# Two-branch attention: PE transposes replaced by normalising in the transposed layout through DRAM, dense pieces re-planned, output projections deferred

## The chip, the cores and the metric

One core of a Trainium2 chip runs the whole program. The metric is the device time of one execution in microseconds (us); the time before is the median of three runs, 526.55 us (526.25 to 527.35).

## What is computed

Two attention branches read their own input of 2048 rows by 640 columns (bf16, 32 heads of 20), and their outputs stand side by side in one 2048 x 1280 result. Cut to what matters:

```
A:  for each of 4 segments s of 512 rows:
      a_dot = softmax(q k^T * scale + causal mask within s) v
      a_mem = (phi(q) M) / (phi(q) z + 1e-6)        # M, z from earlier segments; phi(t) = t+1 if t>0 else exp(t)
      o     = g * a_mem + (1 - g) * a_dot           # g = sigmoid(beta), one per head
      M, z += phi(k)^T v, sum of phi(k)
    out_A = concat(o) @ wo
B:  out_B = softmax over a causal sliding window of 256 keys (q k^T * scale) v @ wo
```

## The kernel before, in words

The work goes in eight phases, B0 A0 B1 A1 B2 A2 B3 A3, one for each branch and chunk of 512 rows. A phase has 20 packs (A, and B0) or 24 packs (B1 to B3); a pack is scored for two pairs of heads. For each pair `scores` (L375) writes a PSUM tile Sc of 128 x 1024 (two of them exist) with matmuls that use 20 rows of the array, ACT takes its exponential into pt (L380, "an exp" below; 344 in all), and DVE (L393, branch B) or POOL (L397, L402) masks blocks of pt. `weigh` (L423) then multiplies by V with four matmuls of 32 columns side by side, into the only tile O. The v tiles carry a column of ones, so that row 20 of each head's group of 32 in O is the softmax's denominator. When a group of four heads (a unit, eight in a phase) is done, DVE copies O to oc (L435), PE transposes oc block by block (L442), and DVE takes the reciprocal of the denominators (L445) and multiplies (L450) into o_tok, which has tokens on the partitions.

Everything else is a list of dense pieces ("atoms") that `run` doles out between the packs, in the proportion of their costs: the projections of the next phase (k and q, five times five matmuls of 512 columns each, L189; v, eight times five of 320 columns, L209), the memory of branch A (phi, L281 to L283; reading M, L306 to L316; transposing phi(k), L326, and updating M, L337 to L348), and the output projection of the phase before (transposing o_tok, L242, copying it, L246, five matmuls of 320 columns each, L253, copying, L256, storing, L260). All of these write PSUM tiles called D, of which there are three; DVE empties them. k and q go through DRAM once to put each head on its own 32 partitions: written by L195 (kd, qd), read back by L200 in four DMAs (kp, qp). Every DMA is issued by SP, in order, and an issue that has to wait holds up all behind it.

The order on each engine is not the order of the code: the tile framework's scheduler fixes a list of instructions for each engine when the program is built, and each engine then works its list off in order. The lists that the section on the change shows are these.

Of the kernel before, what the change touches and what calls it, by code (L numbers as in the profile page):

```python
# [80 lines left out]
class Kern:  # L81

    def __init__(self, ctx, tc, ins, out2d):
# [10 lines left out]
        self.xT, self.qc, self.kc, self.qp, self.kp, self.o_tok = {}, {}, {}, {}, {}, {}  # L94
        self.omem = None
# [12 lines left out]
    def setup(self):  # L108
# [11 lines left out]
        self.w["Aq"] = self.load_w("wAq", ins["A_wq"])  # L120
        self.w["Av"] = self.load_w("wAv", ins["A_wv"])
        self.w["Bo"] = self.load_w("wBo", ins["B_wo"])
        self.w["Ao"] = self.load_w("wAo", ins["A_wo"])
# [13 lines left out]

        bm = cp.tile([P, KT, 8], F32, name="bmask")
        nc.vector.memset(bm[:], 1.0)
        for m in range(KT):  # L140
            off = P * m - DH * (P * m // DH)
            nc.gpsimd.affine_select(out=bm[:, m, :], in_=bm[:, m, :], pattern=[[-DH, 8]],
                                    compare_op=ALU.is_ge, fill=0.0, base=off,
                                    channel_multiplier=1)
            nc.gpsimd.affine_select(out=bm[:, m, :], in_=bm[:, m, :], pattern=[[DH, 8]],
                                    compare_op=ALU.is_ge, fill=0.0, base=DH - 1 - off,
                                    channel_multiplier=-1)
        self.bm = bm
# [20 lines left out]
        self.ge, self.omg = ge, omg  # L169
        self.macc = cp.tile([P, KT, 8, DH + 1], F32, name="macc")  # L170
        self.mz = cp.tile([P, KT, 8, DH + 1], BF16, name="mz")
# [5 lines left out]
    def atoms_qkv(self, br, c):  # L177
# [4 lines left out]
        def proj(which, m):  # L182
            if m == 0:
                t = self.io.tile([P, KT, CH], BF16, name="%sc%s" % (which, br), bufs=1)
                (self.qc if which == "q" else self.kc)[br] = t
# [7 lines left out]
            if m == KT - 1:  # L193
                sc = self.dram.tile([KT * P, CH], BF16, name="%sd%s" % (which, br), bufs=2)
                nc.sync.dma_start(out=sc[:].rearrange("(m p) s -> p m s", p=P), in_=t[:])  # L195
                pt = self.io.tile([P, G, CH], BF16, name="%sp%s" % (which, br),
                                  bufs=2 if (which == "k" and br == "B") else 1)
                src = sc[:].rearrange("(g j d) s -> j d g s", g=G, j=4)
                for j in range(4):
                    nc.sync.dma_start(out=pt[32 * j:32 * j + DH, :, :], in_=src[j])  # L200
                if which == "q":
                    self.qp[br] = pt
                else:
                    self.kp[br, c] = pt
# [21 lines left out]
        for tt in range(CT):  # L226
            for hf in range(2):
                out.append((0.8, lambda tt=tt, hf=hf: vproj(tt, hf)))
        return out

    def atoms_out(self, br, c):
        nc = self.nc
        out = []
        st = {}

        def tr(tt):
            if br == "A" and c > 0 and tt == 0:
                nc.vector.tensor_tensor(out=self.o_tok["A"][:], in0=self.o_tok["A"][:],
                                        in1=self.omem[:], op=ALU.add)
            pT = self.dtile([P, KT, P], BF16)  # L240
            for m in range(KT):
                nc.tensor.transpose(out=pT[:, m, :],  # L242
                                    in_=self.o_tok[br][:, tt, m * P:(m + 1) * P],
                                    identity=self.ident[:])
            oT = self.wk.tile([P, KT, P], BF16, name="oT", bufs=2)
            nc.vector.tensor_copy(out=oT[:], in_=pT[:])  # L246
            st["oT"] = oT
# [318 lines left out]
```

## Time and profile before

| what | value |
|---|---|
| median of three runs | 526.55 us |
| the profiled execution's own time | 526.12 us |
| its span, first to last instruction | 524.0 us |
| busy: PE, DVE, ACT, POOL | 479.0, 348.4, 348.0, 205.3 us |
| mean granted TensorE clock | 0.847 |
| DMA: packets, bytes, share of 16 engines | 52,163, 38.71 MB, 27.7% |

The span is what the views below divide up; the execution's own time has another 2.1 us around it. "Busy" of PE counts overlapping matmuls once. A phase begins with its first exp; in the profile that is at 40.3, 90.9, 142.9, 202.3, 266.7, 327.5, 392.0 and 450.8 us, and the last exp ends at 503.0. The granted clock is 1.00 or 0.50 at any moment, and a stretch's figure is the mean of these.

### The profile page before, as it was taken

The numbers are of one execution on the slowest core, as the hardware profiler recorded it, in microseconds if no ns is written. First come the engines' busy times: TensorE is split into PE (matmuls) and PEld (weight loads), VectorE is DVE, ScalarE is ACT, GpSimd is POOL, SyncE is SP. The second block draws the span as 40 slices with busy tenths as digits, with TensorE's granted clock in tenths as the row PEclk, the third lists the DMA queues.
The fourth block names the chain that finished last, engine by engine and source line by source line (L and its number), as shares of the span: only waits on it lengthen the run. The fifth ranks groups of instructions, "written<-read, shape, count | busy, mean of one in ns | idle before, by whom it ended". The sixth has DMA issues, their size and how long they took to land.

```text
span 524.0 us, 10856 instructions
## 1 busy us (share of the span) xinstructions
PE 479.0 (91%) x4182; PEld 210.8 (40%) x4208; DVE 348.4 (66%) x886; ACT 348.0 (66%) x376; POOL 205.3 (39%) x498
## 2 busy tenths in 40 slices
PE   3947999999998999999999899999999899999975
PEld 1522234345533444454443344344453344433323
DVE  2753569557589996565579997556649977743343
ACT  0016669578789878675479878667448968977630
POOL 1002223346455444453345345344325544554420
PEclk9985569999999799995699789997589979955568
DMA  8993303454113230431013421150010430000001
GB/s 245 322 224 62 100 2 102 81 142 83 45 41 99 71 77 26 137 88 29 14 39 99 102 53 39 64 135 18 1 40 23 115 78 28 26 0 14 27 13 51
DMA packets 52163, 38.71 MB, mean 74 GB/s; under 512 B 22416, under 2 KB 52112, under 8 KB 52112
## 3 DMA queue, kind: packets, MB, share of 16 engines
q1 hardware_dynamic: 52112, 38.03, 27.7%
q8 instruction: 33, 0.54, 0.4%
q14 instruction: 18, 0.15, 0.1%
HBM read 17.05 MB, written 15.73 MB: 63 GB/s over the span
## 4 chain that ended last, share of the span: by engine, by line
PE 69%; DVE 17%; ACT 6%; DMA 4%; issue 2%; SPq 1%; POOL 0%; ACTq 0%; DVEq 0%
PE Sc L375 18%; PE D L189 13%; PE D L253 11%; PE O L423 11%; PE D L209 6%; ACT pt L380 6%; DVE pt L393 5%; PE D L442 4%; DVE oc L435 3%; DVE phi L283 2%; DMA qdB<-qcB 2%; PE D L337 1%; DVE qcA L192 1%; PE D L242 1%; PE D L326 1%
## 5 line engine op out<-in xcount | busy, mean ns | idle before, releaser
L380 ACT ACTIVATE pt<-Sc 128x1024 bf16<-128x1024 f32 (+1 forms) x344 | 332.0, 1015 | 125.2 <-PE Sc L375 88.7
L402 POOL TENSOR_SCALAR_AFFINE_SELECT pt<-pt 128x256 bf16<-128x256 bf16 x224 | 103.0, 470 | 163.8 <-ACT pt L380 158.4
L397 POOL TENSOR_SCALAR_AFFINE_SELECT pt<-pt 128x256 bf16<-128x256 bf16 x256 | 99.8, 408 | 134.1 <-ACT pt L380 130.5
L393 DVE TENSOR_TENSOR pt<-pt,cmask 128x256 bf16<-128x256 bf16 x256 | 79.9, 338 | 26.8 <-ACT pt L380 26.5
L375 PE MATMUL Sc<-qpB,kpB 20*128 20x384 bf16 (+1 forms) x704 | 78.5, 297 | 12.4 <-DMA qpB<-qdB 7.6
L375 PE MATMUL Sc<-qpA,kpA 20*128 20x256 bf16 (+3 forms) x512 | 79.0, 348 | 3.4 <-ACT pt L380 3.1
L256 DVE CAST ot<-D 128x320 bf16<-128x320 f32 x64 | 31.3, 489 | 37.9 <-PE D L253 37.9
L423 PE MATMUL O<-pt,vB 128*32 128x384 bf16 (+2 forms) x720 | 45.5, 299 | 7.4 <-DVE oc L435 5.1
L435 DVE CAST oc<-O 128x512 bf16<-128x512 f32 x64 | 43.6, 681 | 7.9 <-PE O L423 7.6
L375 PEld LDWEIGHTS <-kpB 20*128 20x128 bf16 x704 | 22.4, 94 | 64.5 <-issue 59.1
L423 PE MATMUL O<-pt,vA 128*32 128x256 bf16 (+3 forms) x576 | 45.5, 336 | 0.3 <-DVE oc L435 0.3
L253 PEld LDWEIGHTS <-oT 128*128 128x128 bf16 x320 | 31.1, 109 | 27.6 <-DVE oT L246 9.7
L445 DVE RECIPROCAL rr<-D 128x16 f32<-128x16 bf16 x64 | 16.2, 253 | 34.7 <-PE D L442 33.9
L375 PEld LDWEIGHTS <-kpA 20*128 20x128 bf16 x512 | 19.1, 95 | 43.2 <-issue 38.4
L253 PE MATMUL D<-wBo,oT 128*128 128x320 bf16 x160 | 33.6, 363 | 0.4 <-DVE oT L246 0.4
L189 PE MATMUL D<-xTB,wBk 128*128 128x512 bf16 x94 | 25.0, 403 | 9.3 <-DMA wBk<-in_B_wqkv_dram 9.0
L253 PE MATMUL D<-wAo,oT 128*128 128x320 bf16 x160 | 29.3, 323 | 4.1 <-DVE oT L246 4.0
L209 PE MATMUL D<-wAv,xTA 128*128 128x320 bf16 x160 | 32.0, 346 | 0.0
L442 PE MATMUL D<-ident,oc 128*128 128x128 bf16 x256 | 30.4, 243 | 0.8 <-DVE oc L435 0.8
L189 PE MATMUL D<-xTA,wAq 128*128 128x512 bf16 x92 | 28.1, 430 | 0.6 <-issue 0.3
L423 PEld LDWEIGHTS <-vB 128*32 128x32 bf16 x720 | 14.3, 96 | 35.3 <-issue 16.9
L192 DVE CAST kcB<-D 128x512 bf16<-128x512 f32 x20 | 13.8, 691 | 19.4 <-PE D L189 18.8
(64 smaller groups left out, 461.2 us busy)
## 6 DMA issues: line engine op xcount, KB each, us to landing
out_dram<-ot SPq DMA_DIRECT2D x32, 160.0 KB
kdB<-kcB SPq DMA_DIRECT2D x4, 640.0 KB
qdB<-qcB SPq DMA_DIRECT2D x4, 640.0 KB
kpB<-kdB SPq DMA_DIRECT2D x16, 160.0 KB
qpB<-qdB SPq DMA_DIRECT2D x16, 160.0 KB
kdA<-kcA SPq DMA_DIRECT2D x4, 640.0 KB
kpA<-kdA SPq DMA_DIRECT2D x16, 160.0 KB
qdA<-qcA SPq DMA_DIRECT2D x4, 640.0 KB
```

The source lines that it names most:

```text
L189: nc.tensor.matmul(ps[:], lhsT=self.w[br + which][:, kt, m * P:(m + 1) * P], rhs=self.xT[br][:, kt, :], start=(kt == 0), stop=(kt == KT - 1))
L209: nc.tensor.matmul(ps[:, 0:320], lhsT=self.xT[br][:, kt, tt * P:(tt + 1) * P], rhs=self.w[br + "v"][:, kt, hf * 320:(hf + 1) * 320], start ...
L253: nc.tensor.matmul(ps[:, 0:320], lhsT=st["oT"][:, m, :], rhs=self.w[br + "o"][:, m, hf * 320:(hf + 1) * 320], start=(m == 0), stop=(m == K ...
L256: nc.vector.tensor_copy(out=st["ot"][:, hf * 320:(hf + 1) * 320], in_=ps[:, 0:320])
L375: nc.tensor.matmul(ps[:, i, off * P:(off + nq) * P], lhsT=kp[rows, u.g, k0:k0 + P], rhs=self.qp[u.br][rows, u.g, q0 * P:(q0 + nq) * P], st ...
L380: nc.scalar.activation(out=pt[:, :, 0:pk.used], in_=ps[:, :, 0:pk.used], func=ACT.Exp, scale=SCALE)
L393: nc.vector.tensor_tensor(out=blk, in0=blk, in1=self.cmask[:].unsqueeze(1).to_broadcast([P, 2, P]), op=ALU.mult)
L397: nc.gpsimd.affine_select(out=blk, in_=blk, pattern=[[0, 2], [1, P]], compare_op=ALU.is_ge, fill=0.0, base=0, channel_multiplier=-1)
L402: nc.gpsimd.affine_select(out=blk, in_=blk, pattern=[[0, 2], [-1, P]], compare_op=ALU.is_ge, fill=0.0, base=-1, channel_multiplier=1)
L423: nc.tensor.matmul(u.O[32 * j:32 * j + 32, (q0 + b) * P:(q0 + b + nb) * P], lhsT=v[:, kt % CT, 4 * u.g + j, :], rhs=pk.pt[j // 2][:, j % 2 ...
L435: self.nc.vector.tensor_copy(out=oc[:], in_=u.O[:])
L442: nc.tensor.transpose(out=tp[:, b, :, :].rearrange("p j c -> p (j c)"), in_=u.oc[:, b * P:(b + 1) * P], identity=self.ident[:])
```

## The change

- The softmax's result is no longer transposed on PE. O, unnormalised, is copied into half tiles of four units (`to_half`); `put_half` writes their denominators and numerators to DRAM in eight DMAs; `invert` reads the 32 x 512 denominators back, takes the reciprocal on DVE and writes it to DRAM with every row repeated 20 times in float32 (rex, 640 x 512). `combine` fetches the numerators in the layout of the output projection's stationary operand (oT), loads rex row block by row block (rx) and multiplies on DVE. Only the last unit chunk, A3, still goes through PE transposes (`normalise`, `last_out`).
- The memory of branch A is read in the same layout: four matmuls of 32 x 32 tiles and 512 columns for each of the eight units, then the same way through DRAM. phi(k) is written to DRAM and comes back through a DMA transpose (ktok) in place of PE transposes; the update is eight times four matmuls of 84 columns, and its diagonal blocks are collected by four DMAs.
- The output projections are planned later (`OUTS`, by the phase's number from 0): B0 with B1's pieces, A0 and B1 with B2's, A1 with B3's, and B2, A2 and B3 with A3's.
- `plan` gives each dense piece and each small step a position between 0 and 1 in its phase; `run` issues it when the packs have come that far.
- k's padded tile of branch B is split into halves (three of them), pt has 6 buffers instead of 8, qc and kc share three buffers, and four weights (Aq, Av, Bo, Ao) are loaded behind the first k and q.

DMA issues by SP rise from 129 to 494.

What the change does to the lists of the engines is seen on DVE, which empties PE's dense tiles, and on SP. First DVE in phase B1, before: masks of pt, copies of the dense tiles of the next phase's projections (kcA, qcA), and the normalisation (rr, ot) stand in turns.

```order
L393 TENSOR_TENSOR pt<-pt,cmask 128x2x128
L192 CAST kcA<-D 128x512
L393 TENSOR_TENSOR pt<-pt,cmask 128x2x128 x4
L192 CAST kcA<-D 128x512
L435 CAST oc<-O 128x512
L393 TENSOR_TENSOR pt<-pt,cmask 128x2x128 x2
L192 CAST kcA<-D 128x512
L393 TENSOR_TENSOR pt<-pt,cmask 128x2x128
L445 RECIPROCAL rr<-D 128x16
L450 TENSOR_TENSOR otB<-D,rr 128x4x80
```

The changed kernel on DVE at the end of A0, ahead of B1's first mask (oc are the units of A0, vB and qkc the projections):

```order
L471 CAST oc<-O 128x512 x5
L387 COPY st<-D 80x336
L218 CAST vB_97<-D 128x16x20 x4
L194 CAST qkc<-D 128x512 x7
L354 TENSOR_SCALAR pe<-pe 128x512
L355 SCALAR_TENSOR_TENSOR phi<-qkc,pe 128x512
```

And in B1 itself:

```order
L427 TENSOR_TENSOR pt<-pt,cmask 128x2x128 x3
L471 CAST oc<-O 128x512
L427 TENSOR_TENSOR pt<-pt,cmask 128x2x128 x8
L471 CAST oc<-O 128x512
L427 TENSOR_TENSOR pt<-pt,cmask 128x2x128 x8
L471 CAST oc<-O 128x512
```

The ten copies of A1's k and q projections (qkc) and the eight of its v, which stood between the masks of B1, now stand in one run between the last copy of A0's O and the first mask of B1. PE's list reads the same: between the scores of A0 and of B1 lie 32 update matmuls, 20 of B1's v, 50 of A1's k and q and 40 of A1's v, without a score; in the 192 score matmuls of B1 there is no dense one.

The second place is SP ahead of phase A2, which needs kpA and qpA. Before:

```order
L195 DMA kdA<-kcA 128x5x512
L200 DMA kpA<-kdA 20x8x512 x4
L195 DMA qdA<-qcA 128x5x512
L200 DMA qpA<-qdA 20x8x512 x4
L100 DMA_TRANSPOSE xTA<-in_A_x_dram 128x5x512
```

After (dn reads A1's denominators back, rexA_3486 is A1's repeated reciprocal, rx and oT belong to the outputs of A0 and B1):

```order
L268 DMA dn<-denA_3048 32x128 x4
L197 DMA kdA_3583<-qkc 128x5x512
L284 DMA oT<-numA_1323 128x5x512
L278 DMA rexA_3486<-ri 640x1x128 x4
L237 DMA kpA<-kdA_3583 20x8x512 x4
L290 DMA rx<-rexA_1716 128x512
L197 DMA qdA_3772<-qkc 128x5x512
L290 DMA rx<-rexA_1716 128x512 x2
L284 DMA oT<-numB_2171 128x5x512
L237 DMA qpA<-qdA_3772 20x8x512 x4
```

kpA and qpA now stand behind the four issues of rexA, which wait for a reciprocal (ri) on DVE; and DVE's list has that reciprocal behind the last copy of O of phase B2:

```order
L427 TENSOR_TENSOR pt<-pt,cmask 128x2x128 x8
L471 CAST oc<-O 128x512
L275 RECIPROCAL ri<-dn 128x128
L292 TENSOR_TENSOR oT<-oT,rx 128x512 x5
L320 CAST ot<-D 128x320 x4
```

The same holds ahead of A3; ahead of A1 the reciprocal stands in the middle of B1.

The diff, cut to its core:

```diff
-        self.w["Aq"] = self.load_w("wAq", ins["A_wq"])
...
-                t = self.io.tile([P, KT, CH], BF16, name="%sc%s" % (which, br), bufs=1)
+                t = self.io.tile([P, KT, CH], BF16, name="qkc", bufs=3)
...
+    def put_half(self, key, hf, oc):
...
+        for j in range(4):
+            nc.sync.dma_start(out=dv[j][:, gs, :], in_=oc[32 * j + DH:32 * j + DH + 1, :, :])
+        for j in range(4):
+            nc.sync.dma_start(out=nv[j][:, gs, :], in_=oc[32 * j:32 * j + DH, :, :])
+    def invert(self, key):
...
+        for q in range(4):
+            nc.sync.dma_start(out=dn[32 * q:32 * q + 32, :], in_=dv[q])
...
+            nc.vector.reciprocal(out=ri[:], in_=dn[:])
...
+        for q in range(4):
+            nc.sync.dma_start(out=rv[q],
+                              in_=ri[32 * q:32 * q + 32, :].unsqueeze(1).to_broadcast([32, DH, P]))
...
+    def scale_rows(self, key, m):
+        nc = self.nc
+        r = self.wk.tile([P, CH], F32, name="rx", bufs=2)
+        nc.sync.dma_start(out=r[:], in_=self.rex[key][m * P:(m + 1) * P, :])
+        t = self.oT[key]
+        nc.vector.tensor_tensor(out=t[:, m, :], in0=t[:, m, :], in1=r[:], op=ALU.mult)
...
+    def read(self, c, g):
+        nc = self.nc
+        ps = self.dtile([P, CH], F32)
+        for j in range(4):
+            nc.tensor.matmul(ps[32 * j:32 * j + 32, :], lhsT=self.mz[32 * j:32 * j + DH, g, :],
+                             rhs=self.pq[32 * j:32 * j + DH, g, :], start=True, stop=True,
+                             tile_position=(32 * j, 32 * j))
+        self.to_half("M%d" % c, g, ps)
...
-        pt = self.wk.tile([P, 2, CH], BF16, name="pt", bufs=8)
+        pt = self.wk.tile([P, 2, CH], BF16, name="pt", bufs=6)
...
+    OUTS = {2: ["B0"], 4: ["A0", "B1"], 6: ["A1"], 7: ["B2", "A2", "B3"]}
+    def plan(self, n, phases):
...
+        for cost, f in dense:
+            pos.append((lead + (0.97 - lead) * at / total, f))
+            at += cost
...
+            spread(self.combine(key), max(0.0, t - 0.3), max(0.0, t - 0.05))
...
+        for i, (_, f) in enumerate(self.atoms_qkv("B", 0)):
             f()
+            if i == 2 * KT - 1:
+                for name in ("Aq", "Av", "Bo", "Ao"):
+                    self.w[name] = self.load_w("w" + name, self.ins["%s_w%s" % tuple(name)])
...
-                goal = total * (i + 1) / np_
-                while atoms and done + 0.5 * atoms[0][0] <= goal:
-                    cost, f = atoms.pop(0)
-                    f()
-                    done += cost
+                while atoms and atoms[0][0] < (i + 1.0) / len(ph.packs):
+                    atoms.pop(0)[1]()
```

More of the change, by code (lines that the diff above doesn't have):

```diff
@@ L136, in setup @@
         self.cmask = cmask
[L138 to L148, printed above, removed]
         vs = {}
@@ L356, in atoms_mem @@
[L356 to L363 removed]
+        st = self.wk.tile([GW, 4, 4, W], F32, name="st", bufs=1)
+        nc.vector.tensor_copy(out=st[:], in_=ps[0:GW])
+        for j in range(4):
+            nc.sync.dma_start(out=self.dm[32 * j:32 * j + DH, 4 * hf:4 * hf + 4, :],
+                              in_=st[DH * j:DH * j + DH, :, j, :])
```

359 lines of the change are left out of this document (194 added, 165 removed).

## The prediction

> **What bounds the kernel now.** I read the busy time by phase first (stretch; length; busy us of PE, PEld, DVE, ACT and POOL with counts; granted clock; DMA share; GB/s). The rows are the start, B0, B1, A1, A3 and the end:
>
> ```profile
> 0.00:40.30 40.30, 23.48 (x112) 11.43 (x114) 20.12 (x41) 4.08 (x7) 2.53 (x18) 0.95 0.98 260
> 40.30:90.90 50.60, 45.81 (x345) 16.91 (x349) 32.92 (x97) 35.97 (x42) 14.18 (x32) 0.67 0.27 66
> 142.90:202.30 59.40, 56.01 (x572) 23.77 (x572) 52.57 (x141) 51.49 (x58) 29.52 (x66) 0.94 0.26 68
> 202.30:266.70 64.40, 63.08 (x533) 29.56 (x532) 37.59 (x97) 39.07 (x40) 24.94 (x65) 0.81 0.24 62
> 450.80:503.00 52.20, 51.00 (x394) 19.74 (x386) 22.46 (x58) 39.54 (x40) 24.32 (x63) 0.59 0.04 14
> 503.00:524.00 21.00, 11.92 (x89) 6.96 (x88) 9.78 (x19) 0.00 (x0) 0.77 (x2) 0.81 0.11 40
> ```
>
> Between the start, where the DMA is full (0.98), and the end, PE fills every phase: 56.01 of 59.40 us, 63.08 of 64.40, 51.00 of 52.20. ACT comes second, and it can be busy that much only because scores and dense pieces alternate on PE. Next the costliest groups, for what ACT needs and what the change takes off PE and DVE (count; busy us, mean ns; idle before):
>
> ```profile
> L380 ACT ACTIVATE pt<-Sc 128x1024 bf16<-128x1024 f32 (+1 forms) x344 | 332.0, 1015 | 125.2 <-PE Sc L375 88.7 <-POOL pt L397 14.1 <-POOL pt L402 10.2
> L442 PE MATMUL D<-ident,oc 128*128 128x128 bf16 x256 | 30.4, 243 | 0.8 <-DVE oc L435 0.8
> L242 PE MATMUL D<-ident,otB 128*128 128x128 bf16 x80 | 9.1, 259 | 0.0
> L242 PE MATMUL D<-ident,otA 128*128 128x128 bf16 x80 | 7.7, 232 | 2.4 <-DVE otA L238 2.4
> L326 PE MATMUL D<-ident,phi 128*128 128x128 bf16 x60 | 7.3, 278 | 0.0
> L306 PE MATMUL D<-mz,phi 128*128 128x21 bf16 (+3 forms) x120 | 10.3, 215 | 0.0
> L337 PE MATMUL D<-vA,pkt 128*128 128x147 bf16 (+1 forms) x60 | 8.3, 295 | 0.0
> L445 DVE RECIPROCAL rr<-D 128x16 f32<-128x16 bf16 x64 | 16.2, 253 | 34.7 <-PE D L442 33.9
> ```
>
> Last the clock, in short stretches, and what it does to one piece, in the order of time (start us, us):
>
> ```profile
> 45.00:50.00 5.00, 4.64 (x35) 1.25 (x30) 2.33 (x9) 4.57 (x6) 1.43 (x4) 0.50 0.01 2
> 450.80:456.00 5.20, 4.98 (x70) 2.45 (x62) 3.74 (x13) 5.20 (x6) 3.04 (x9) 1.00 0.09 32
> 466.00:471.00 5.00, 5.00 (x34) 1.73 (x32) 2.35 (x7) 3.07 (x3) 2.26 (x6) 0.50 0.00 0
> ```
> ```profile
> 255.95 2.74 PE L253 MATMUL D<-wBo,oT 128*128 128x320 bf16 x10
> ...
> 259.73 1.53 PE L253 MATMUL D<-wBo,oT 128*128 128x320 bf16 x10
> ...
> 497.26 0.61 PE L375 MATMUL Sc<-qpA,kpA 20*128 20x512 bf16 x2
> 497.80 0.62 PE L423 MATMUL O<-pt,vA 128*32 128x384 bf16 x8
> 498.35 0.61 PE L375 MATMUL Sc<-qpA,kpA 20*128 20x512 bf16 x2
> ```
>
> At 0.50 ten matmuls of the output projection take 2.74 us, at 1.00 they take 1.53. PE was busy all of 466 to 471 and the clock stayed at 0.50: scores (20 rows of the array) and O (32 columns) do not bring it up; runs of whole-array matmuls do. A step of scores costs 0.54 us there (497.26 to 497.80), one of O 0.55.
>
> **The change, and what it takes off.** 224 of 256 transposes of oc go (30.4 x 224/256 = 26.6 us), 140 of 160 of o_tok (16.8 x 140/160 = 14.7), and L326's 7.3. L306 and L337 (18.6) are replaced by 24 groups of four matmuls and 96 updates: by the O row (eight in 0.55, cold; half that warm) and L337's mean spacing (8.3/60), between 14 and 21, say 16. That is 26.6 + 14.7 + 7.3 + 18.6 - 16 = 51 us of PE work. DVE loses most of L445 and of the two groups behind it, and gets fifty multiplications; its 348 us are not the bound. If PE's order had stayed, the gain would be some 40 to 50 us.
>
> It has not stayed. In the lists shown above the pieces that filled PE while ACT worked stand in blocks between the phases: B1 and B3 have no dense piece, and of the dense matmuls behind the start 268 of 512 columns and 421 of 320 lie in some thirteen blocks without a score. In a block ACT runs dry, since two Sc tiles are all it has in hand; in a score stretch PE waits for ACT. Their times add, where they overlapped before.
>
> **The sum, stage by stage.**
>
> *Start, 44 us (42 to 45).* PE's list has all of A0's projections in front of B0's scores, where 20 matmuls stood.
>
> ```profile
> 16.21 5.34 PE L189 MATMUL D<-xTB,wBq 128*128 128x512 bf16 x24
> ...
> 21.61 5.60 PE L209 MATMUL D<-wBv,xTB 128*128 128x320 bf16 x40
> 22.53 1.18 SPq L195 DMA_DIRECT2D qdB<-qcB  x1
> 30.12 1.51 SPq L200 DMA_DIRECT2D kpB<-kdB  x4
> ```
>
> From 27.2 (21.61 + 5.60) come 50 x 0.2225 (5.34/24) = 11.1 and 40 x 0.14 (5.60/40) = 5.6: 43.9, against 40.3. The DMA is no later: two of twelve loads move behind qp, and at 260 GB/s the rest, some 9 MB, is in by 35.
>
> *Exps, 349 us (332 to 363).* 332.0 us if ACT never waits. In 45 to 50, scores and O nearly alone at 0.50, ACT had 4.57 of 5.00 (332/0.914 = 363); in 450.8 to 456 at full clock all of it. Cold, a pack of two exps asks of PE two steps of scores and one or more of O, 0.54 x 2 + 0.55 = 1.63 us against ACT's 1.93 (2 x 332/344). So ACT bounds these stretches at either clock, but with little room: 0.95 of it, 349.
>
> *Blocks, 128 us (118 to 145).* 268 x 0.2225 = 59.6; 421 x 0.14 = 58.9; 96 updates 10; 21 groups of reads at 0.33 7; together 135.5. At each beginning ACT still works off what is in Sc, 0.6 us x 13 = 8.
>
> *Cold starts, 15 us (0 to 25).* Ten blocks come out of a score stretch; each loses about what 2.74 against 1.53 shows, 1.2 to 2 us.
>
> *Waits for DMAs, 44 us (10 to 95).* Not in the trace of before: SP's list is now long, and PE waits behind it at four places. Prices: four issues of 1.18 (640 packets each, as qd; rex has as many) are 4.7, four loads of kp 1.51, and the landing of 640 KB in quiet by SP's own waits:
>
> ```profile
> SPq L200 <- DMA kdA<-kcA: 12.3, 4, 3.2
> ```
>
> 12.3/4 = 3.1. *A2's first score*: the reciprocal comes behind B2's last copy of O, then rex 4.7, kp 1.5, qd 1.2, three rx and an oT some 2.3, qp 1.5, landing 3.1: 14 us, in which PE has nothing in its list before A2's scores. *A3*: rex 4.7, kp and qp 3.0, landing 3.1: 11. *The reads of memory in A1 and A2*: pq stands behind rex of the B phase before; 4.7 + 1.5 + 3.1 and a reciprocal, some 10, less the five matmuls and four exps that PE's list has there: 7 each. *A3's outputs*: B2's multiplications stand behind rex of B3, some 5. Sum 44; nothing is covered by less than 0 (then 10 for what must land), and if each goes through a full queue, as kd did in the start (landing 10 us), it doubles.
>
> *Dense pieces left in the score stretches, 8 us (0 to 20).* 32 wide ones in B0, about 95 of 320 columns elsewhere; cold 0.27 each, mostly inside the 0.15 us by which ACT is slower per exp.
>
> *End, 20 us (17 to 24).* 21.00 before; the memory's addition to all of o_tok goes, and its last chain through DRAM comes before the last outputs.
>
> 44 + 349 + 128 + 15 + 44 + 8 + 20 = 608 us of span. The profiled execution had 2.1 us around its span of 524.0, and its 526.1 is 0.4 under the median: **610 us**.
>
> **The page against the trace.** The Trainium skill's "TensorE: Matmul & The Clock Gate" (Part 1, What's actually happening) has the clock open fully after one busy window of about 3.4 us and close only after an idle one. Here 466 to 471 is busy 5.00 of 5.00 at 0.50, so the trace does not bear that out for these narrow matmuls. By that rule the score stretches, with PE busy over 60%, would be warm, and the sum would be the first rival's.
>
> **Rivals.** *The score stretches are warm*: a step of scores at half of 0.54, ACT without waits: 332 in place of 349, no cold starts, no remainder of dense pieces: 608 - 17 - 15 - 8 = 568, 570 with what lies around. For it: 450.8 to 456, 1.00 with ACT at 5.20 of 5.20. Against it: 45 to 50 and 466 to 471. 0.15.
>
> *SP's queue bounds*: 494 issues in order, many waiting for landings; the four waits at their upper ends, 95: 608 + 51 = 659, 661. For it: kd landed only 10 us after its issue when the DMA was full. Against it: 0.04 to 0.27 of DMA share in the phases, and about twice the packets would leave half of it free. 0.16.
>
> *Faster: ACT alone bounds, back to back.* Exps follow one another closer than their mean when nothing holds them:
>
> ```profile
> 45.90 4.59 ACT L380 ACTIVATE pt<-Sc 128x1024 bf16<-128x1024 f32 x5 [0.43 <-PE Sc L375]
> ```
>
> With a mean length of 1.015 that is (4.59 - 1.015)/4 = 0.89 apart. With 344 x 0.92 = 316, blocks at 118, the end at 17 and no wait, 44 + 316 + 118 + 17 = 495, 497. It decides from where exps, cold starts, remainders and waits together stay under 524 - 44 - 118 - 17 = 345; my middle has 416. Against it: 45 to 50, where ACT waited. 0.07. Within 0.2% (about what a measurement of this kernel can tell from no change): 0.02.
>
> **Chances.** The forecast has 0.60, its own range is 575 to 640. The range of 555 to 665 takes in the first rival and the middle of the second. Faster 0.07, same 0.02, slower 0.91. The likeliest case gives 610.
>
> **What would show it.** In the profile after: ACT's idle before L414 waiting for PE's scores near 200 us instead of 88.7; stretches of 20 to 30 us at the end of A0, and inside A1 and A2, with ACT nearly idle and PE at 1.00; B1 to B3 near 50 us each with ACT over 0.9 busy and the clock at 0.50; PE's busy sum lower by some 50 us if the clock were equal, hidden by cold scores; PE waiting for kpA, qpA and pqA by name. I am wrong if scores and dense matmuls alternate in B1, or if ACT is busy in the blocks.

## The result and the profile after

The changed kernel takes 760.8 us, the median of four runs (758.3 to 763.1), against 526.4 us for the kernel before (521.4 to 527.4): a ratio of 1.448, with a 95% interval of 1.438 to 1.458. The prediction was 610 us, with a range of 555 to 665. The sign was right; the size was far out.

First the busy time by stretches of the profiled execution, whose span is 757.8 us (columns as in the prediction's first view: busy us of PE, PEld, DVE, ACT and POOL, granted clock, DMA share, GB/s). The rows are the start, B1, a stretch inside A1 without scores, B2, the time between B2's last exp and A2's first, and the end.

```profile
0.00:43.10 43.10, 34.61 (x182) 18.00 (x184) 28.39 (x60) 4.86 (x8) 1.08 (x8) 1.00 0.97 253
...
174.80:229.30 54.50, 47.10 (x374) 12.62 (x375) 24.21 (x76) 47.62 (x48) 29.31 (x63) 0.53 0.52 121
...
279.50:327.30 47.80, 34.90 (x210) 15.63 (x215) 28.44 (x53) 6.13 (x11) 2.00 (x3) 0.79 0.57 134
343.50:397.50 54.00, 47.14 (x374) 12.51 (x375) 24.59 (x76) 47.58 (x48) 29.77 (x63) 0.52 0.22 57
397.50:426.50 29.00, 4.78 (x19) 1.20 (x17) 3.92 (x6) 0.01 (x1) 0.52 (x1) 0.50 0.70 170
...
720.40:757.80 37.40, 12.22 (x81) 7.61 (x78) 13.95 (x28) 0.04 (x1) 0.77 (x2) 0.68 0.35 101
```

The picture is the predicted one. B1 and B2 hold nothing but scores, O and exps, at half clock; in the stretch inside A1 ACT is busy 6 of 48 us. The sizes are not: B1 and B2 take 54 us with ACT 0.87 and 0.88 busy, not over 0.9; the stretch inside A1 is 48 us long at a mean clock of 0.79, not 20 to 30 at 1.00; and in the 29 us ahead of A2 no engine does anything to speak of, while the DMA engines are 0.70 busy. The profile has no such row before the change.

Then the groups of exps and of O, the changed kernel's first and the kernel before's O behind them (count; busy us, mean ns of one; idle before):

```profile
L414 ACT ACTIVATE pt<-Sc 128x1024 bf16<-128x1024 f32 (+1 forms) x344 | 336.3, 1014 | 233.6 <-PE Sc L409 164.6 <-PE O L457 58.7 <-POOL pt L431 2.3
...
L457 PE MATMUL O<-pt,vB 128*32 128x384 bf16 (+2 forms) x720 | 93.6, 399 | 21.0 <-DVE pt L427 12.5 <-POOL pt L436 8.0 <-DVE oc L471 0.3
...
L457 PE MATMUL O<-pt,vA 128*32 128x256 bf16 (+3 forms) x576 | 69.3, 379 | 14.5 <-POOL pt L431 8.0 <-DVE oc L471 5.2 <-DVE oc L482 0.7
```
```profile
L423 PE MATMUL O<-pt,vA 128*32 128x256 bf16 (+3 forms) x576 | 45.5, 336 | 0.3 <-DVE oc L435 0.3
L423 PE MATMUL O<-pt,vB 128*32 128x384 bf16 (+2 forms) x720 | 45.5, 299 | 7.4 <-DVE oc L435 5.1 <-DVE pt L393 1.7
```

The same 1296 matmuls of O keep PE busy for 163 us instead of 91. The mean of one has grown by a third and by an eighth (399 ns against 299, 379 against 336), the sum by four fifths: fewer of them run side by side. That was no term of the prediction.

Then PE's longest waits in the changed kernel (us in total, times, longest):

```profile
PE D L317 <- DVE oT L292: 33.6, 6, 18.1
PE Sc L409 <- ACT pt L414: 22.3, 29, 1.2
PE D L317 <- DVE oTt L339: 18.4, 4, 16.4
PE Sc L409 <- DMA oT<-numA: 18.0, 1, 18.0
PE D L370 <- DMA pqA<-phiq: 18.0, 2, 9.6
```

All but the second row wait for something that comes back from DRAM, 88 us together. Where they come from is seen between B2 and A2, in SP's list and PE's:

```profile
400.37 4.60 SPq L278 DMA_DIRECT2D rexA<-ri  x4
405.08 4.09 SPq L237 DMA_DIRECT2D kpA<-kdA  x4
409.21 0.35 SPq L290 DMA_DIRECT2D rx<-rexA  x1
```
```profile
398.15 0.61 PE L457 MATMUL O<-pt,vB 128*32 128x256 bf16 x6 [0.58 <-POOL pt L436]
416.83 0.98 PE L317 MATMUL D<-wAo,oT 128*128 128x320 bf16 x3 [18.07 <-DVE oT L292]
```

A1's four writes of rex go out, then kp, and only then a load of rx. That load belongs to A0's output (rexA_1716 in SP's list, in the section on the change) and needs nothing of these writes: it stands behind them in the list. The multiplication and PE's output matmul follow, and PE has stood for 18.07 us.

The times of the exps divide the span in a way that can be set against the prediction's sum: the start up to the first exp, the stretches in which exps follow one another, the gaps of over 2.5 us between exps, and the end behind the last exp.

| us | start | stretches | gaps | end | span |
|---|---|---|---|---|---|
| predicted | 44 | 349 + 8 = 357 | 128 + 15 + 44 = 187 | 20 | 608 |
| changed kernel | 43.1 | 402.2 | 275.1 (17 gaps) | 37.4 | 757.8 |
| kernel before | 40.3 | 451.3 | 11.4 (3 gaps) | 21.0 | 524.0 |

So 45 us too few were put on the stretches, 88 on the gaps and 17 on the end.

### The profile page after: what moved, and what is told of

Read it like the earlier page. It is cut to its first block, busy times and chain, and to the rows that moved or that the text cites. A ratio compares the mean times of both kernels' runs of the same rounds, so it can differ in the third digit from the quotient of the medians.

```text
span 757.8 us, 10341 instructions
## 1 busy us (share of the span) xinstructions
PE 571.1 (75%) x3782; PEld 205.0 (27%) x3796; DVE 330.4 (44%) x731; ACT 356.5 (47%) x377; POOL 215.4 (28%) x488
## 4 chain that ended last, share of the span: by engine, by line
PE 59%; DVE 11%; DMA 11%; ACT 7%; SPq 5%; issue 4%; POOL 1%; DVEq 0%; ACTq 0%; POOLq 0%
PE Sc L409 17%; PE O L457 16%; PE D L191 12%; PE D L317 7%; ACT pt L414 6%; PE D L212 5%; DVE oc L471 4%; SPq L278 3%; DMA qpA<-qdA 3%; PE D L370 2%; DMA pqA<-phiq 2%; DMA rx<-rexM 1%; SPq L237 1%; DVE phi L355 1%; DMA qdA<-qkc 1%
## 5 line engine op out<-in xcount | busy, mean ns | idle before, releaser
L431 POOL TENSOR_SCALAR_AFFINE_SELECT pt<-pt 128x256 bf16<-128x256 bf16 x256 | 108.7, 444 | 318.3 <-ACT pt L414 317.3
L436 POOL TENSOR_SCALAR_AFFINE_SELECT pt<-pt 128x256 bf16<-128x256 bf16 x224 | 105.6, 481 | 187.0 <-ACT pt L414 186.9
L409 PE MATMUL Sc<-qpA,kpA 20*128 20x128 bf16 (+3 forms) x512 | 87.7, 407 | 41.4 <-DMA oT<-numA 18.0
L409 PE MATMUL Sc<-qpB,kpB 20*128 20x384 bf16 (+1 forms) x704 | 106.4, 397 | 6.8 <-ACT pt L414 4.8
L457 PE MATMUL O<-pt,vB 128*32 128x384 bf16 (+2 forms) x720 | 93.6, 399 | 21.0 <-DVE pt L427 12.5
L457 PE MATMUL O<-pt,vA 128*32 128x256 bf16 (+3 forms) x576 | 69.3, 379 | 14.5 <-POOL pt L431 8.0
L194 DVE CAST qkc<-D 128x512 bf16<-128x512 f32 x80 | 55.2, 690 | 51.8 <-PE D L191 51.7
L292 DVE TENSOR_TENSOR oT<-oT,rx 128x512 bf16<-128x512 bf16 x50 | 35.3, 717 | 87.6 <-DMA rx<-rexA 58.7
L353 ACT ACTIVATE pe<-qkc 128x512 bf16<-128x512 bf16 x30 | 18.8, 630 | 111.4 <-DVE qkc L194 98.4
L457 PEld LDWEIGHTS <-vA 128*32 128x32 bf16 x576 | 20.1, 101 | 67.5 <-issue 61.2
L191 PE MATMUL D<-xTB,wBq 128*128 128x512 bf16 x96 | 33.7, 486 | 2.4 <-DVE oc L471 1.6
```

The costliest lines, as they stand in the source:

```text
L191: nc.tensor.matmul(ps[:], lhsT=self.w[br + which][:, kt, m * P:(m + 1) * P], rhs=self.xT[br][:, kt, :], start=(kt == 0), stop=(kt == KT - 1))
L194: nc.vector.tensor_copy(out=t[:, m, :], in_=ps[:])
L292: nc.vector.tensor_tensor(out=t[:, m, :], in0=t[:, m, :], in1=r[:], op=ALU.mult)
L409: nc.tensor.matmul(ps[:, i, off * P:(off + nq) * P], lhsT=kp[rows, u.g, k0:k0 + P], rhs=self.qp[u.br][rows, u.g, q0 * P:(q0 + nq) * P], st ...
L431: nc.gpsimd.affine_select(out=blk, in_=blk, pattern=[[0, 2], [1, P]], compare_op=ALU.is_ge, fill=0.0, base=0, channel_multiplier=-1)
L436: nc.gpsimd.affine_select(out=blk, in_=blk, pattern=[[0, 2], [-1, P]], compare_op=ALU.is_ge, fill=0.0, base=-1, channel_multiplier=1)
```

## The experiments

The theory from here: two causes that add. One is the order of PE's list: dense pieces in blocks, and O's four matmuls in two pairs. The other is the trip of the reciprocals through DRAM. The rivals are the half clock by itself, and each of the two causes alone.

Single runs of the kernel before lay between 520 and 549 us in these sessions, and four runs of one changed version between 636 and 657; where versions have one run each, differences below some 30 us are read as none.

### All engines in the order of the code

The changed kernel, and the kernel before as its control, with every instruction put in the order in which the code writes it:

```
-    with _tile.TileContext(nc) as tc:
+    with _tile.TileContext(nc, linearize=True) as tc:
```

(and the sizes of five pools in the changed kernel).

> The changed kernel with every engine's instructions in the order of its code, in which a dense piece stands behind every few scores (the largest run of dense matmuls between two scores is 21 instead of 194) and O's four matmuls stay together; some pools are resized for it (oT 3, pt 7, pe, ot and oTt 1). Every DMA, wait chain and multiplication of the change is still there. Theory 1, the order of PE's list (blocks without scores, O split in pairs, a cold clock between the blocks) cost the time: 520 to 600 us, PE busy below 500, no clock below 0.7 in a phase. Theory 2, the normalisation's round trips through DRAM on SP's queue cost it: they stay, 680 us or more, with PE waiting for qpA, kpA and oT about as long as now.

> Control: the kernel before with its instructions in the order of its code (largest run of dense matmuls between scores 24). Theory 1 needs that the order of the code is no slower by itself: 515 to 545 us. If it gives over 560, a time of the changed kernel in that order can't be set against 526.

Measured: 2968 us, and the control 2255. The busy times of the first:

```profile
PE 702.3 (24%) x3765; PEld 204.3 (7%) x3796; DVE 349.8 (12%) x731; ACT 369.4 (12%) x377; POOL 197.2 (7%) x488
```

The busy times of PE, DVE, ACT and POOL add up to 55% of the span (in the control 76%): hardly anything overlaps, since with this option an instruction waits for the one written before it on whatever engine. Both numbers are near sums of latencies and say nothing on either theory. The runs below that pin PE alone replace them.

### O's four matmuls kept together

```
-            for j in range(4):
-                nc.tensor.matmul(u.O[32 * j:32 * j + 32, ...
+            for i, j in enumerate((2, 3, 0, 1)):
+                mm = nc.tensor.matmul(u.O[32 * j:32 * j + 32, ...
+                if i:
+                    self.tc.keep_in_program_order(mm)
```

> The changed kernel with O's four matmuls of a weigh pinned to follow one another; the blocks stay (dense matmuls in blocks 858 instead of 904). Theory 1a, the pairs cost a full step each and make PE the bound of the score stretches: L457's (O) busy sum falls from 163 us to 95 to 120, exps follow one another at 1.0 us instead of 1.09 to 1.23, the time falls by 30 to 50 us to 710 to 730. Theory 1b, scores alone at half clock bound these stretches: O's busy time falls, but the exps stay at 1.1 or more and the time falls by less than 15 us. Theory 2 (DRAM waits) gives no change either.

Measured: 725.5 us, 35 less. O's groups in this run:

```profile
L457 PE MATMUL O<-pt,vB 128*32 128x384 bf16 (+2 forms) x720 | 61.2, 400 | 8.6 <-POOL pt L436 4.5 <-DVE pt L427 1.9 <-DVE oc L473 0.3
L457 PE MATMUL O<-pt,vA 128*32 128x256 bf16 (+3 forms) x576 | 47.9, 378 | 7.5 <-DVE oc L473 3.5 <-POOL pt L431 2.7 <-DVE oc L484 0.7
```

109 us, as theory 1a said (95 to 120), at the same mean of one matmul as in the changed kernel. Here is PE in B2, the changed kernel first and this one behind it:

```profile
365.55 0.61 PE L409 MATMUL Sc<-qpB,kpB 20*128 20x384 bf16 x4
366.70 0.48 PE L457 MATMUL O<-pt,vB 128*32 128x384 bf16 x1 [0.54 <-DVE pt L427]
367.11 0.61 PE L409 MATMUL Sc<-qpB,kpB 20*128 20x384 bf16 x4
367.64 0.61 PE L457 MATMUL O<-pt,vB 128*32 128x384 bf16 x7
```
```profile
344.32 0.60 PE L409 MATMUL Sc<-qpB,kpB 20*128 20x384 bf16 x4
344.85 0.62 PE L457 MATMUL O<-pt,vB 128*32 128x256 bf16 x8
345.40 1.24 PE L409 MATMUL Sc<-qpB,kpB 20*128 20x384 bf16 x8
```

In the first, O follows each step of scores, here with one matmul and then with the other seven (two and six in most packs of B2), and once waits 0.54 us for DVE's mask, the scores behind it waiting too. In the second, O's eight matmuls come in one step, and one step of O serves two of scores. B2's 48 exps go from 343.5 to 397.5 in the changed kernel, 1.13 us apart, and from 325.3 to 373.9 here: 1.01, which is what the prediction had taken (349/344). The pairs were the cause there. Over the whole kernel the stretches in which exps follow one another, divided as in the table above, fall from 402.2 to 377.5 us, 25 of the 45 that were too few; the other 20 were not parted. And B2 of this run, in the columns as above, is at half clock too:

```profile
325.30:373.90 48.60, 41.26 (x371) 11.14 (x371) 24.48 (x76) 46.20 (x48) 29.79 (x63) 0.52 0.25 63
```

ACT is busy 46.20 of its 48.60 us: with O kept together, the half clock alone does not make PE the slower one in a stretch of scores.

### TensorE's matmuls held in the order of the code

A wrapper pins each matmul and transpose behind the one written before it; the other engines and all waits stay the scheduler's. (In these runs all of PE's instructions carry the wrapper's line, L109 or L110.)

```
+    def pinned(self, f):
+        def g(*a, **k):
+            r = f(*a, **k)
+            self.tc.keep_in_program_order(r)
+            return r
+        return g
```

> The changed kernel with TensorE's matmuls alone held in the order of its code, each behind the one written before it; all other engines, every DMA, wait and buffer stay as the change has them. Nothing waits for anything that it did not need, unlike in the run before in which every instruction waited for its predecessor on whatever engine. The largest block of dense matmuls without a score is 21 instead of 194, and O's four matmuls stay together. Theory 1, the order of PE's list costs the time: 0.97 to 1.12 of the kernel before, exps overlapped with dense pieces, mean clock above 0.75. Theory 2, the round trips through DRAM cost it: 1.25 of the kernel before or more, with PE's scores waiting for qpA and its output matmuls for oT for over 150 us in sum.

> Control: the kernel before with TensorE's matmuls held in the order of its code. By theory 1 the order in which this kernel ran is near that of its code (largest block 24 against none of 20), so 0.97 to 1.08 of the kernel before. If it comes out over 1.10, pinning costs time by itself, and the pinned changed kernel can't be set against 1.

Measured: 648.1 us (median of four runs, 636 to 657), 1.23 times the kernel before (648.1/526.6; the two shortest runs alone give 640 us and 1.22); the control gave 549.2, the upper end of what the unchanged kernel gave, so pinning by itself costs at most some 23 us. The result lies between both theories' numbers, and each holds its part: 113 us went with the order, and the rest did not. PE's busy time and clock in this run, and then its waits:

```profile
PE 455.4 (71%) x3765; PEld 178.6 (28%) x3796; DVE 334.2 (52%) x731; ACT 345.9 (54%) x377; POOL 209.4 (33%) x488
...
PEclk9956978988978997995576798667855557659757
```
```profile
PE D L109 <- DVE oT L310: 62.2, 10, 26.9
PE D L109 <- DVE oT L306: 38.5, 11, 16.3
PE D L109 <- DVE oTt L353: 15.1, 4, 13.0
```

PE is busy 455 us instead of 571 with the same matmuls, at a mean clock of 0.77 instead of 0.65, and idle for 116 us while it waits for oT and oTt: with the blocks gone, nothing stands between a late oT and PE.

### Without the reciprocals' trip

rex is neither written nor read; the denominators still come back and the reciprocals are taken, but the rows are multiplied by 1, so these kernels leave the normalisation out. Once in the changed kernel (a_norex), once pinned (a_pin_norex):

```
-        for q in range(4):
-            nc.sync.dma_start(out=rv[q], in_=ri[32 * q:32 * q + 32, :]...)
...
-        nc.sync.dma_start(out=r[:], in_=self.rex[key][m * P:(m + 1) * P, :])
+        nc.gpsimd.memset(r[:, 0:1], 1.0)
```

> The changed kernel without rex: the reciprocals are taken but not written to DRAM, and the rows are multiplied by a constant 1 (the normalisation is left out). 36 writes of 640 short packets and 60 loads of rx go from SP's queue; the blocks stay (dense matmuls in them 832 instead of 904). Theory 1: the waits that go are those in front of A2, A3, A3's outputs and the end, 30 to 70 us of 758; 690 to 730 us. Theory 2, these round trips are what the change costs: the time falls below 640.

> The pinned changed kernel without rex (as a_norex: the normalisation is left out, the rows are multiplied by 1). Theory 1 + 2, order of PE's list and round trips are two causes and nothing else matters: PE's waits for oT and oTt in the pinned run (27, 41, 21 and 15 us, 104 in sum) go, 648 - 104 = 544 us, within 0.99 to 1.06 of the kernel before. Rival, the reciprocals' trip is hidden again behind another wait (pq, kpA, numB): 590 us or more, with PE waiting for one of these. Rival 3, something else in the change costs (narrow matmuls, deferred outputs): above 590 with PE busy.

Measured: 674.6 us, 86 less than the changed kernel: more than theory 1's 30 to 70 and less than the 120 that theory 2 asked for. (The kernel has forty writes of rex and fifty loads of rx, not 36 and 60.) And 539.0 us pinned, 109 less, where 544 was expected. Order and trip together take 222 of the 234 us between the kernels. PE in the last run:

```profile
PE 450.8 (84%) x3765; PEld 177.7 (33%) x3796; DVE 328.0 (61%) x731; ACT 345.0 (64%) x377; POOL 218.4 (41%) x538
```
```profile
PE D L109 <- DVE oT L307: 8.8, 4, 5.4
...
PE D L109 <- DVE oTt L350: 2.6, 4, 0.7
```

The waits for oT fell from 116 to 11 us. The 12 us left to the kernel before are below what single runs tell. PE is busy 28 us less than in it (450.8 against 479.0), and the time is no shorter; why wasn't tried. None of the versions run here beats the kernel before.

### The half clock by itself

One, then two matmuls of the whole array into each Sc tile ahead of its scores, which overwrite them:

```
         ps = self.ps.tile([P, 2, CH], F32, name="Sc", bufs=2)
+        for i in range(2):
+            nc.tensor.matmul(ps[:, i, :], lhsT=self.ident[:], rhs=self.w["Bk"][:, 0, 0:CH],
+                             start=True, stop=True)
```

> The changed kernel with one more matmul of the whole array (128x128 weights, 512 columns) into each Sc tile ahead of its scores, 344 in all, overwritten by them: the work of PE rises by 344 x 0.2225 = 77 us at full clock, 150 at half. Theory 1c, the half clock is what makes the score stretches slow: clock above 0.9 in all of them, score and O steps halve (1.63 us per pack less, some 140 us of PE's time for 77 added), the time falls to 690 to 730. Rival, the number of PE's steps and not the clock bounds: the time rises by 40 to 100 us, to 800 to 860, with the clock up or not.

> The changed kernel with two of the overwritten whole-array matmuls per Sc tile instead of one: 688 x 0.2225 = 153 us of added work at full clock, 0.445 us per exp, near what the kernel before had of dense pieces per exp. With one the clock stayed at 0.67 in the mean. If the share of whole-array work sets the clock, it now holds 1.0 in the score stretches (mean above 0.85) and the time is not above that with one, 847; if the clock does not follow the work on the array, the mean stays below 0.75 and the time is above 930.

Measured: 846.8 us at a mean clock of 0.67, and 870.8 at 0.71. Two stretches of the second, in B1 and in B2 (columns as above):

```profile
210.00:215.00 5.00, 5.00 (x34) 1.06 (x34) 2.12 (x5) 2.73 (x4) 2.22 (x5) 0.50 0.03 10
...
415.00:420.00 5.00, 5.00 (x28) 0.92 (x26) 3.00 (x7) 2.46 (x4) 1.57 (x3) 0.50 0.30 66
```

PE is busy without a break and the clock stays at 0.50. Both expectations that needed a raised clock failed, and with them the test: the clock was not raised, so how much of the pinned run's 113 us comes from the clock and how much from work done at the same time stays open. The rival's number for the first run (800 to 860, more steps, more time) was right; for the second its clock (below 0.75) was right and its time (above 930) was not. The second cost only 24 us more than the first, with the list in another order (O mostly in fours again), so the two are no ladder.

### What in the trip costs the time

Nine more runs, all of the pinned version (648.1 us; without rex 539.0).

**Smaller loads, more buffers.** rex in bf16 and four buffers of rx:

```
-        rx = self.dram.tile([D, CH], F32, name="rex%s" % key)
+        rx = self.dram.tile([D, CH], BF16, name="rex%s" % key)
...
-        r = self.wk.tile([P, CH], F32, name="rx", bufs=2)
+        r = self.wk.tile([P, CH], BF16, name="rx", bufs=4)
```

> The pinned changed kernel with rex in bf16 and four buffers of rx instead of two: each rx load has half the bytes, and four can be under way. The chain of waits of the pinned run shows loads of 2.66 to 2.78 us and multiplications of 0.70 taking turns. If these turns are what PE's output matmuls wait for, the waits for oT fall by half (some 45 us, to 595 to 615). If it is SP standing before a rex write whose reciprocal is not ready, with the loads of an older key behind it, the time falls by less than 20 us (630 to 648).

Measured: 608.9 us, 39 less, inside the first case's numbers. But four things changed in it (bytes written, bytes read, buffers, and a copy of the reciprocals to bf16 on DVE), so the case itself is not shown by it.

**The reciprocal later** (a_pin_inv). `invert` called at 0.4 and 0.93 of a phase instead of with the last unit:

```
-            self.invert(key)
+            self.ready.append(key)
...
+        small += [(0.4, invert_ready), (0.93, invert_ready)]
```

> The pinned changed kernel with the reciprocal and its write to DRAM put off to 0.4 or 0.93 of a phase, when the denominators have long landed: SP then doesn't stand in front of a rex write (15.6 us once in the pinned run, before A1's outputs). If SP's standing is the cause, the waits of 27 and 41 us go and the time falls by 40 to 70 us, to 580 to 610; if the turns of load and multiplication are, it falls by less than 20.

Measured: 656.1 us, no gain. SP's waits in front of the writes of rex, all rows of that line added up, came to 41 us instead of the pinned run's 79. The longest row:

```profile
SPq L293 <- DVE ri L290: 30.2, 5, 11.9
```

So half of the standing went and the time did not fall, which speaks against the standing. It is no clean test, since the writes, and the outputs that need them, come later too.

**The loads alone.** rex written as before, never read; the normalisation is left out:

> The pinned changed kernel with rex still written to DRAM but never read: the rows are multiplied by a constant 1 (the normalisation is left out). It parts the 109 us between the pinned run and the one without rex. If the loads of rx, taken in turns with the multiplications through two buffers, are the cost: 540 to 555 us, all of it gone. If the writes of rex (16 to 20 us of SP's time per phase, 640 packets each) and what stands behind them are the cost: above 610, nearly as the pinned run. In between, both.

Measured: 627.5 us. The loads are worth 20 us, within the spread; 89 of the 109 are in the writes. This overturned what I took from the chain of waits of the pinned run, where loads and multiplications in turns are the most visible pieces.

**A quarter of the packets** (a_pin_wide). The reciprocals in 32 partitions of 512, written by one DMA:

```
-        for q in range(4):
-            nc.sync.dma_start(out=rv[q], in_=ri[32 * q:32 * q + 32, :]...)
+        nc.sync.dma_start(out=rx[:].rearrange("(h d) s -> h d s", d=DH),
+                          in_=ri[:].unsqueeze(1).to_broadcast([H, DH, CH]))
```

> The pinned changed kernel with the reciprocals taken in 32 partitions of 512 instead of 128 of 128: rex then goes out as one DMA of 640 packets of 2 KB per key instead of four with 2560 packets of 512 bytes in all, the same 1.28 MB; the denominators come back in one DMA instead of four; the reciprocal takes some 3 us instead of 0.94. If the number of packets and issues of rex (4.4 us of SP per key, and the landing of what stands behind it, oT 10.4 us once in the run without rx loads) is what costs its 89 us, the time falls by 45 to 85 us, to 560 to 600. If its bytes or its place in the chain cost, it falls by less than 20 or rises.

Measured: 656.0 us, no gain. The reciprocal takes 3.3 us in it instead of 0.94, once for each of ten keys.

**Another queue, or a later write from it.** The writes issued by ScalarE (a_pin_rexact); the whole trip by GpSimd (a_pin_trip_pool); the late reciprocal with ScalarE's writes (a_pin_late_act):

```
-            nc.sync.dma_start(out=rv[q],
+            nc.scalar.dma_start(out=rv[q],
```

> The pinned changed kernel with the writes of rex issued by ScalarE's queue instead of SP's, all else the same: SP no longer stands before a write whose reciprocal isn't ready, nor spends 4.4 us on it, but the packets are the same. If SP's standing and issue time cost the 89 us, the time falls to 570 to 600, less some 40 us that ScalarE now issues for (10 keys by 4.4), partly in its idle time. If the packets in the DMA engines cost it, the time stays within 20 us of the pinned run, 630 to 665, and loads behind them land as late as now.

> The pinned changed kernel with the whole trip of the reciprocals, the loads of the denominators and the writes of rex, issued by GpSimd, the engine with most idle time, instead of SP; the packets are the same. With the writes on ScalarE's queue PE's waits for oT had fallen from 116 to about 30 us, but ScalarE itself stood in front of them (scores waited 55 us for exps). If the order of one queue is the cause, the oT waits stay that small and nothing takes their place but some masks held back: 560 to 610 us. If what the writes do in the DMA engines is the cause, 635 or more.

> The pinned changed kernel with the reciprocal put off (as a_pin_inv) and the writes of rex on ScalarE's queue (as a_pin_rexact): ScalarE should find the reciprocal ready, so its stand of 55 us should mostly go. If a queue's standing is the cause of the 89 us: 580 to 615. If the chain is simply late (each of den, dn, ri, rex and rx waits for the landing of the one before), putting it off makes the outputs later: 650 or more.

Measured, in this order: 652.2, 632.9 and 640.0 us, at most 15 from the pinned version's 648.1, which is read as no difference. The first two should have come down to 600 and 610 us or less if the order of one queue were the cause; the third lies between its two cases. In the run on ScalarE's queue another wait has taken the place of the one that was moved (PE's waits):

```profile
PE Sc L109 <- ACT pt L428: 55.5, 33, 8.7
...
PE D L109 <- DVE oT L310: 13.4, 5, 4.0
```

oT is waited for 13 us instead of 62, and the exps, queued on ScalarE behind writes that wait, 55 instead of 13. The Trainium skill's "DMA: Bandwidth & Descriptors" (Issuing engines are not separate DMA queues) says that DMAs of any issuing engine run on the same 16 DMA engines and that more issuers save only issue time. These three runs agree with it: the packets stayed, and so did the time.

**Standing or packets.** Two runs that keep one each, against the 627.5 us of the run with writes and no loads:

```
-            nc.sync.dma_start(out=rv[q], in_=ri[32 * q:32 * q + 32, :]...)
+        nc.sync.dma_start(out=small[:], in_=ri[:])
```
```
-                              in_=ri[32 * q:32 * q + 32, :].unsqueeze(1)...
+                              in_=self.one[32 * q:32 * q + 32, :].unsqueeze(1)...
```

> The pinned run without rx loads (627.5 us), with each key's four writes of rex (2560 packets, 1.28 MB) replaced by one write of the reciprocals as they are (128 packets, 64 KB, not read), at the same ten places of SP's list and with the same wait for the reciprocal. The normalisation is left out. If SP's standing before a write whose reciprocal isn't ready costs the 89 us: 605 to 630. If the writes themselves cost it: 540 to 565.

> The pinned run without rx loads, with the same forty writes of rex and all their packets taken from a constant tile, so that none waits for a reciprocal; they stand some places earlier in SP's list, and the normalisation is left out. If SP's standing costs the 89 us: 540 to 565. If the writes themselves, their issue time and packets, cost it: 605 to 630. Both near 580 would say that each carries half.

Measured: 552.4 us with the standing and only small writes, 611.6 with the large writes and no standing. In the first SP still stands 73 us in front of the ten small writes (all rows of that line; 90 in the run with the large ones), so the edit kept what it was to keep. The writes themselves are the cause; SP's standing before them carries some 13 us (552.4 - 539.0), within the spread. How they act is seen in the chains of waits of the run with the writes and of the one with small writes, each ahead of a phase of A, where a key's write, kp, qp and oT are issued in turn:

```profile
485.32 6.03 DMA kpA<-kdA
491.37 10.36 DMA oT<-numM
```
```profile
300.51 3.31 DMA kpA<-kdA
303.83 11.05 DMA oT<-numB
```

Behind the large write (issued from 480.63 to 485.2) the first kp lands 6.03 us after its issue, behind the small one (issued at 300.07) after 3.31. oT takes 10 to 11 us in both, so that length is not rex's: kp and qp stand ahead of it. From the write's first issue to the landing of oT it is 21.1 us against 14.8. The difference, 6.3 us for each of ten keys, would be 63 of the 75 us between the two runs; that is an estimate from one place.

And a write of rex itself takes long to land. In the changed kernel's own chain at the end:

```profile
726.29 6.55 DMA rexM<-ri
732.97 2.46 DMA rx<-rexM
736.17 2.54 DMA rx<-rexM
```

That goes by its bytes, 1.28 MB of rex per key, more than by its packets. The same write in the pinned run, in the run with a quarter of the packets, and in the one in bf16, which has half the bytes in as many packets:

```profile
610.48 6.56 DMA rexM<-ri
...
620.49 8.86 DMA rexM<-ri
...
583.27 4.18 DMA rexM<-rb
```

The first and the third row begin with a later one of four issues, the first of which was at 607.68 and 581.19. From the first issue to the last landing it is 9.4, 8.9 and 6.3 us: a quarter of the packets and one issue instead of four changed little, half the bytes took a third off. How much of the 39 us that bf16 and four buffers gained comes from the shorter writes was not parted.

## Why the prediction was wrong

The steps, in the order of its sum.

*The change part by part, and the shape.* Right in kind. PE's work fell (busy 455 us in the pinned run against 479; the sum's 51 can't be checked on runs with different clocks), the list came out in blocks, ACT ran dry in them, and every named place of a wait was there: A2's first score, A3's, the reads of memory, A3's outputs, the end.

*Start, 44 us.* Right: 43.1.

*Exps, 349 us, "ACT bounds these stretches at either clock".* **This step failed.** It took "two steps of scores and one or more of O" per pack, 1.63 us against ACT's 1.93. In the change's order most packs have two steps of O, one behind each step of scores, since two of the four matmuls need only the first pt; with 0.54 x 2 + 0.55 x 2 = 2.18 us PE is the slower one (measured in B2: 2 x 1.13 = 2.26), and its O also waits for masks. The rows had the length of a step; how many steps there are stood in the order of PE's list, which I had read for blocks and not for the length of O's runs. Keeping the four together gave 35 us and, in B2, the predicted spacing of 1.01. Measured: 402 us for stretches (with the dense pieces left in them) against 357, and 378 with the four kept together: the pairs are 25 of the 45 us.

*Blocks 128 and cold starts 15.* Under-priced. Without the trip, the change's order still has 193 us of gaps between exps (the run of 674.6 us), against 143. In these gaps PE is busy 172 us, some 73 of them at half clock (worked out from each gap's busy time and granted clock). At full clock that work would take about 136 us, 8 above the sum's 128; the half clock adds 36 instead of 15; and for 21 us PE stands idle, for which the sum had nothing here.

*Waits for DMAs, 44 us, upper end 95.* **The second step that failed**, in its likely value; the upper end held. In the change's order the gaps are 82 us shorter without the trip (275.1 - 192.9) and the end 13 (37.4 - 24.4): 95 in all, of which 86 show in the time, since the start and the stretches are 10 us longer in that run. The price of rex was 4.7 us of SP's issue time, plus 3.1 for a load landing in quiet. Its 1.28 MB were left out: a write lands after 6.6 us, the four issues of kp behind it take 4.1 instead of the priced 1.5, and the first kp lands after 6.0 instead of 3.3. At A2's first score the exps stop for 29.0 us where the sum had 14, at A3's for 21.4 where it had 11. The run with small writes shows that the writes, and not the queue's standing, are what PE waits for.

*End, 20 us.* 37.4. The step said that the memory's last chain "comes before the last outputs". The rows above show it ending the kernel: rex 6.55 us, then loads and multiplications in turns, and PE waits 16.4 us for the first oTt. Without the trip the end is 24.4.

With these the sum closes (the terms are the differences of the table, so this checks the division and not the causes): 608 + 45 (stretches) + 50 (blocks) + 51 (DMA waits, 95 instead of 44) + 4 (the end without the trip, 24.4 against 20) = 758, against a span of 757.8.

*The rivals.* "SP's queue bounds", 661 us, had the place right and the carrier wrong: the DMA engines' bytes, not SP's order. That it was set beside the forecast instead of on top of it is the error of the range: the two causes are nearly independent (113 us and 86 us each by itself, 222 together), and both came out high. "The score stretches are warm" is refuted by B1 and B2 at 0.53 and 0.52. "Faster" fell with ACT waiting 234 us.

## What to carry to other kernels

When a scheduler has reordered a list, count the steps per unit of work in it, not only where pieces have moved: four matmuls that run side by side cost one step together and two in pairs. Price a write by its bytes in the DMA engines and by what is queued behind it, also where that needs nothing of it, and not by its issue time. Where several terms can each come out high for reasons of their own, the range's upper end is a sum of them, not the largest.

## What was not expected of the hardware

The granted clock stayed at 0.50 with PE busy 5.00 of 5.00 us while two matmuls of the whole array per Sc tile stood between scores and O; the mean was 0.50 from 205 to 260 us, in B1, and 0.51 from 400 to 460, in B2. The prediction had read from the trace that runs of whole-array matmuls bring it up; interleaved two by two, they do not. The Trainium skill's "TensorE: Matmul & The Clock Gate" (Part 1, What's actually happening) ties the clock to how busy PE has been in a window of some 3.4 us; the trace, by the busy time that its profile counts, does not agree for this mixture either. The added matmuls had the identity as weights, and whether others, or longer runs of them, would raise the clock wasn't tried.
